# Sliding-window attention with sinks and a two-layer MLP on one core: the transpose of one pair moved from TensorE to the DMA, the second chunk's work in a new order, and attention slots placed one by one

## The chip, the cores and the metric

The kernel runs on one core of one Trainium2 chip. The metric is the device time in microseconds of one execution, as the median of several. The execution that the profile records has a *span* (first to last recorded instruction) that is about 2 us shorter than its device time; all times of a trace are counted from the span's start. Some executions run at a lowered TensorE clock; they are marked slow and no difference is read from them.

## The reference, cut to what matters

```python
scores = q @ k.T / sqrt(64)               # 4 batches, 8 heads, 768 tokens, 64 wide
keep = (key < 4) | (0 <= query - key < 128)      # 4 sinks, a window of 128
a = softmax(where(keep, scores, -1e9)) @ v
x = a.transpose(0, 2, 1, 3).reshape(3072, 512)
out = gelu(x @ w_in) @ w_out              # w_in 512 x 2048, w_out 2048 x 512
```

## The kernel before: the parts that matter

Tokens go in *pairs* of two blocks of 128 (pair 0 to 11); two pairs make a *chunk* of 512 tokens (0 to 5). For a chunk, gemm 1 multiplies x by W_in (gelu follows), and gemm 2 multiplies by W_out. While gemm 2 of one chunk runs, the attention of the next is put between its matmuls. For chunks 1 to 4 a loop does this. For chunk 0, with all the loads of the start, a list OPS written by hand says in which order all engines get their work; its last part is gemm 2 of chunk 0 with the attention of chunk 1 (pairs 2 and 3), called *the second chunk's attention* below.

```python
STREAM = [("k", 0), ("q", 0), ("v", 0), ("k", 1), ...]    # order of the loads; q, k, v of pairs 4 to 11 follow
OPS = [ ...
    ("T", [3,0], "V"), ("s", [2,2], ""), ("m", [2,2], ""), ("s", [2,3], ""),
    ("g2", [[0,6],[1,6],[0,7],[1,7]], ""), ("T", [3,1,1], "VA"), ("av", [2,0,2], ""),
    ("g2", [[0,8],[1,8],[0,9],[1,9]], ""), ("xT", [2,0], "V"), ("s", [3,0], ""),
    ... ]
```

"take" casts a loaded tile to bf16 (V = VectorE, A = ScalarE, G = GpSimd), "T" transposes q or k, "s" is one score with its exponential, "m" its mask on VectorE, "av" attention times v, "xT" the transpose of the attention output into x, "h" a quarter of gemm 1, "g2" four matmuls of gemm 2, "tab" a table load of ScalarE. A *filler* is a matmul whose result nobody uses; the *eviction* is the copy of finished output rows ("osb") out of the tile that the matmuls write.

A pair named in an "xT" gets its x by TensorE and a copy; any other by one crossbar transpose (a DMA transfer that transposes on its way) on the DMA queue of SyncE:

```python
    X_PE = {op[1][0] for op in OPS if op[0] == "xT"}
    ...
            if g in X_PE:                       # at the end of av
                PO[g, p] = po
            elif DONE[g] == NPAIR:
                o = 2 * (g % 2)
                nc.sync.dma_start(out=xt_tile(g // 2)[:, o : o + 2]..., in_=XG[g]..., transpose=True)
    ...
            elif name == "take":                # in run(OPS)
                take(tuple(args), *engs)
                pump(where["q", 6])             # issue loads up to pair 5's, as far as buffers are free
    ...
        n = 0                                   # chunks 1 to 4: where attention goes in
        LEAD = [6] + [8] * (len(att) - 2) + [10]
        for s in range(len(mms)):
            gemm2_mm(c, *mms[s])
            if n < len(att) and 2 * s >= 7 * n + LEAD[n]:
                for w in att[n]:
                    w()
                n += 1
```

Loads and crossbar transposes share one queue, so a transpose stands behind the loads issued before it.

The softmax here doesn't subtract the row's maximum and nothing guards it: scores larger than these inputs give would overflow.

## Time and profile before

225.46 us (median of 3, 225.24 to 225.54); with one more run at the time of the comparison, 225.35.

| Start of (us from the span's start) | before |
|---|---|
| first W_in matmul of chunk 0 | 21.43 |
| last W_in matmul of chunk 0 | 37.59 |
| first W_out matmul of chunk 0 | 38.92 |
| gemm 1 of chunks 1 to 5 | 59.99, 93.71, 126.47, 159.29, 192.78 |
| last copy of an output | 220.69 |
| end of the span | 223.60 |

The starts come from the single matmuls of the trace; the chain of waits starts a piece where the one before it ends, some 0.17 us later. TensorE is busy 96% of the span, so the table is a list of stages of one engine, and a gain is a stage that got shorter. The lines behind it stand in the prediction below.

### The profile page before, as it was taken

Reading aid. Unit: us, or ns where it says so; the run is one execution under the profiler, and the core shown is the slowest. Engines: PE = TensorE matmul, PEld = TensorE weight load, DVE = VectorE, ACT = ScalarE, POOL = GpSimd, SP = SyncE. Lnnn points to the kernel's source line nnn. Section 1 sums busy time; section 2 is a strip of 40 time slices with the busy share of each in tenths; the row PEclk is TensorE's granted clock in tenths of the full one; section 3 lists DMA queues with packets and bytes.
Section 4 is the critical chain, followed back from the end, with each engine's and each line's share of the span. In section 5 each row is a group of like instructions: output and inputs, shape, how many; then the busy total and the mean of one; then the engine's idle time right before and its main releaser. Section 6 shows DMA issues by size and latency. Waiting matters only on the chain.

```text
span 223.6 us, 4228 instructions
## 1 busy us (share of the span) xinstructions
PE 215.2 (96%) x1705; PEld 114.7 (51%) x1705; DVE 112.8 (50%) x267; ACT 120.8 (54%) x148; POOL 52.3 (23%) x97
## 2 busy tenths in 40 slices
PE   7798999999999999999999999999999999999994
PEld 2355887554544465444455444455444465444454
DVE  4438825887591188391188480288560297100121
ACT  2367675856255976055974065964156973177100
POOL 8475413546030011220011310011400011300100
PEclk9999999999999999999999999999999999999999
DMA  6999999999487995567995477996493026510022
GB/s 171 290 348 388 355 352 288 343 291 308 163 170 128 256 295 124 115 140 114 297 295 100 94 153 152 299 243 98 99 176 54 3 47 97 117 23 3 5 89 94
DMA packets 70066, 40.11 MB, mean 179 GB/s; under 512 B 27168, under 2 KB 64416, under 8 KB 70048
## 3 DMA queue, kind: packets, MB, share of 16 engines
q1 hardware_dynamic: 67824, 34.02, 61.4%
q0 software_dynamic: 2080, 5.77, 10.2%
q8 instruction: 13, 0.21, 0.4%
q10 hardware_dynamic: 144, 0.07, 0.1%
q14 instruction: 5, 0.04, 0.1%
HBM read 27.26 MB, written 6.29 MB: 150 GB/s over the span
## 4 chain that ended last, share of the span: by engine, by line
PE 85%; ACT 5%; DVE 4%; DMA 2%; issue 1%; SPq 0%; DVEq 0%
PE po L682 34%; PE big L613 29%; PE bank L546 4%; PE big L473 4%; PE big L646 4%; ACT et L482 3%; DMA st<-in_q_dram 2%; PE po L646 2%; PE bank L613 2%; PE bank L526 1%; ACT L715 1%; DVE et L490 1%; DVE xg L568 1%; PE qkps L363 1%; PE big L462 1%
## 5 line engine op out<-in xcount | busy, mean ns | idle before, releaser
L682 PE MATMUL po<-WOUT,gt 128*128 128x512 bf16 (+2 forms) x416 | 89.8, 364 | 0.1
L613 PE MATMUL big<-xt,WIN 128*128 128x512 bf16 x300 | 66.1, 379 | 0.0
L682 PEld LDWEIGHTS <-gt 128*128 128x128 bf16 x416 | 36.9, 98 | 38.9 <-issue 3.0
L632 ACT ACTIVATE gt<-big 128x1024 bf16<-128x1024 f32 (+1 forms) x32 | 30.6, 969 | 44.1 <-PE big L613 44.1
L613 PEld LDWEIGHTS <-WIN 128*128 128x128 bf16 x320 | 31.3, 98 | 37.8
L482 ACT ACTIVATE et<-big 128x1024 bf16<-128x1024 f32 (+1 forms) x48 | 43.4, 952 | 11.8 <-PE big L473 11.6
L697 POOL DMA_DIRECT2D out_dram<-osb x40 | 22.9, 578 | 107.8 <-DVE rz L564 79.9
L490 DVE TENSOR_TENSOR et<-et,mask 128x1024 bf16<-128x1024 bf16 x31 | 22.6, 739 | 33.6 <-ACT et L482 33.2
L272 DVE COPY osb<-po 128x512 f32<-128x512 f32 (+2 forms) x25 | 16.1, 645 | 39.2 <-PE po L682 39.2
L568 DVE TENSOR_TENSOR xg<-bank,rz 128x256 bf16<-128x256 f32 x44 | 18.7, 424 | 1.5
L546 PEld LDWEIGHTS <-et 128*128 128x128 bf16 x352 | 15.2, 97 | 4.9 <-DVE et L490 0.7
L272 DVE CAST vo<-st 64x512 bf16<-64x512 f32 x36 | 16.4, 457 | 0.4
L473 PE MATMUL big<-qt,kt 64*128 64x128 bf16 (+1 forms) x256 | 15.6, 238 | 0.8 <-ACT et L482 0.2
L546 PE MATMUL bank<-vo,et 128*128 128x65 bf16 x324 | 15.1, 193 | 0.6 <-DVE et L490 0.6
L626 ACT ACTIVATE gt<-big 128x1024 bf16<-128x1024 f32 (+1 forms) x8 | 9.8, 1243 | 10.7 <-PE big L613 10.7
L646 PEld LDWEIGHTS <-WIN 128*128 128x128 bf16 x128 | 12.3, 98 | 1.5
L473 PEld LDWEIGHTS <-kt 64*128 64x128 bf16 x256 | 8.6, 94 | 7.6 <-issue 6.0
L497 DVE TENSOR_TENSOR et<-et,mask 128x768 bf16<-128x768 bf16 x12 | 6.9, 579 | 10.0 <-ACT et L482 9.6
L715 ACT ACT_TABLE_LOAD x9 | 11.5, 1283 | 0.2
L646 PE MATMUL big<-xt,WIN 128*128 128x256 bf16 x80 | 10.3, 273 | 0.0
L564 DVE RECIPROCAL rz<-bank 128x4 f32<-128x4 f32 x44 | 7.7, 175 | 4.6 <-PE bank L546 3.8
L272 DVE CAST k<-st 128x1024 bf16<-128x1024 f32 (+1 forms) x12 | 8.0, 669 | 3.3 <-DMA st<-in_k_dram 3.2
(87 smaller groups left out, 142.8 us busy)
## 6 DMA issues: line engine op xcount, KB each, us to landing
st<-in_k_dram SPq DMA_DIRECT2D x12, 512.0 KB, 7.3
st<-in_q_dram SPq DMA_DIRECT2D x12, 512.0 KB, 7.2
st<-in_v_dram SPq DMA_DIRECT2D x12, 512.0 KB, 7.2
out_dram<-osb POOLq DMA_DIRECT2D x40, 128.0 KB, 2.7
st<-in_moe_w_in_dram SPq DMA_DIRECT2D x8, 512.0 KB, 9.4
st<-in_moe_w_out_dram SPq DMA_DIRECT2D x8, 512.0 KB, 8.8
out_dram<-osb POOLq DMA_DIRECT2D x2, 256.0 KB, 2.3
kt<-k SPq DMA_TRANSPOSE x16, 3.0
```

The lines of the kernel that those rows point to most:

```text
L272: eng.tensor_copy(out=out, in_=in_)
L473: nc.tensor.matmul(ps[:, hl, c : c + n * P], lhsT=kt(gk, p, ek, rows), rhs=qt(g, p, e, n, rows), start=not add, stop=True, skip_group_chec ...
L482: nc.scalar.activation(out=et[:, :, c0:], in_=ps[:, :, c0:], func=AF.Exp, scale=att_scale)
L490: nc.vector.tensor_tensor(out=et.rearrange("p h (e n) -> p (h e) n", e=2), in0=et.rearrange("p h (e n) -> p (h e) n", e=2), in1=mask.unsqu ...
L546: nc.tensor.matmul(pos[n][:, e * PV + hl * DV : e * PV + (hl + 1) * DV], lhsT=ets[n][:, hl, c : c + P], rhs=vo[:, h, :], start=e == 0 and ...
L568: nc.vector.tensor_tensor(out=XG[g][:, :, 2 * p : 2 * p + 2, :], in0=po[:, 0 : 2 * PV].rearrange("p (e h c) -> p e h c", e=2, h=2)[:, :, : ...
L613: nc.tensor.matmul(outs[a], lhsT=WIN[:, t, ts(f, P)], rhs=XT[c][:, :, t, :], start=(t == 0), stop=(t == NKT - 1),)
L632: nc.scalar.activation(out=gt.rearrange("k a n -> k (a n)"), in_=src, func=AF.Gelu)
L646: nc.tensor.matmul(out4[a], lhsT=WIN[:, t, ts(f, P)], rhs=XT[c][:, 2 * half : 2 * half + 2, t, :], start=(t == 0), stop=(t == NKT - 1), sk ...
L682: nc.tensor.matmul(po, lhsT=GT[c, f // 4][:, f % 4, ts(m, P)], rhs=WOUT[:, f, cols], start=(f == 0), stop=(f == NFT - 1),)
L697: nc.gpsimd.dma_start(out=out[r0 : r0 + P, :].rearrange("(s r) c -> r s c", r=2)[r], in_=osb[HP * r : HP * (r + 1), :],)
L715: nc.scalar.activation(out=warm[:, 1:2], in_=warm[:, 0:1], func=func)
```

## The change

Its intent: eight transposes less for TensorE, and fewer moments in which it waits in the second chunk's attention and at the later chunks' scores. The diff without most of the reordered list:

```diff
 STREAM = [
-    ("k", 0), ("q", 0), ("v", 0), ("k", 1), ("q", 1), ("v", 1), ("wi", 0), ("wi", 1), ("wi", 3),
+    ("k", 0), ("q", 0), ("v", 0), ("k", 1), ("q", 1), ("wi", 0), ("v", 1), ("wi", 1), ("wi", 2),
...
-    ("wo", 1), ("wo", 0), ("k", 2), ("v", 2), ("q", 3), ("k", 3), ("wo", 4), ("wo", 5),
+    ("wo", 2), ("k", 2), ("wo", 0), ("q", 3), ("v", 2), ("k", 3), ("wo", 4), ("wo", 5),
 OPS = [
... (the head: other engines for casts and copies, two products later)
-    ("T", [3,0], "V"), ("s", [2,2], ""), ("m", [2,2], ""), ("s", [2,3], ""),
-    ("g2", [[0,6],[1,6],[0,7],[1,7]], ""), ("T", [3,1,1], "VA"), ("av", [2,0,2], ""),
-    ("g2", [[0,8],[1,8],[0,9],[1,9]], ""), ("xT", [2,0], "V"), ("s", [3,0], ""),
+    ("T", [3,0], "V"), ("s", [2,2], ""), ("g2", [[0,4],[1,4],[0,5],[1,5]], ""),
+    ("s", [2,3], ""), ("m", [2,2], ""), ("g2", [[0,6],[1,6],[0,7],[1,7]], ""),
+    ("T", [3,1,1], "V"), ("g2", [[0,8],[1,8],[0,9],[1,9]], ""), ("av", [2,0,2], ""),
... (("xT", [2,0..3]) are gone)
+    SLOT = [3, 12, 19, 26, 33, 41]
+    def ahead():
+        return where["q", 6 if 2 in X_PE or DONE.get(2) == NPAIR else 5]
...
-                pump(where["q", 6])
+                pump(ahead())
...                                            (after av)
+                pump(ahead())
...
-        n = 0
-        LEAD = [6] + [8] * (len(att) - 2) + [10]
-        for s in range(len(mms)):
-            gemm2_mm(c, *mms[s])
-            if n < len(att) and 2 * s >= 7 * n + LEAD[n]:
-                for w in att[n]:
+        for n, mm in enumerate(mms):
+            gemm2_mm(c, *mm)
+            if att and n in SLOT:
+                for w in att[2 * SLOT.index(n)]:
                     w()
-                n += 1
```

`ahead()` holds the loads of pair 5 until the transpose of pair 2 has been issued. The old loop's filled slots lay after matmuls 3, 11, 18, 25, 32 and 40.

## The prediction

> **What bounds the kernel now.** I read the page first, then the table of stretches, the chain of waits in order of time, what the matmuls waited for, and last the timelines of single engines around the waits found.
>
> ```profile
> PE 215.2 (96%) x1705; PEld 114.7 (51%) x1705; DVE 112.8 (50%) x267; ACT 120.8 (54%) x148; POOL 52.3 (23%) x97
> L613 PE MATMUL big<-xt,WIN 128*128 128x512 bf16 x300 | 66.1, 379 | 0.0
> ```
>
> Only TensorE is full. But 379 ns for a 128x512 matmul is not its cost: matmuls overlap. The chain gives the true price, 32 of them in 6.91 us, so 216 ns each. With that price I went through the starts of all matmuls of the trace and counted as lost only what exceeds columns/2.4 GHz + 2.5 ns.
>
> ```profile
> 7.00:15.00 8.00, 7.23 (x83) 4.20 (x83) 4.20 (x10) 4.36 (x7) 4.99 (x9) 1.00 1.17 309
> 15.00:24.00 9.00, 8.01 (x99) 5.29 (x94) 6.39 (x15) 6.91 (x10) 5.54 (x7) 1.00 1.05 387
> 24.00:37.50 13.50, 13.50 (x150) 12.16 (x149) 6.18 (x14) 8.16 (x13) 4.42 (x5) 1.00 1.10 327
> 37.50:60.16 22.66, 21.82 (x209) 11.55 (x207) 16.40 (x38) 14.57 (x23) 9.78 (x14) 1.00 0.99 296
> 60.16:74.20 14.04, 14.04 (x66) 6.34 (x65) 7.68 (x15) 7.65 (x8) 2.63 (x4) 1.00 0.74 137
> ```
>
> Columns: length, then busy time of TensorE, its weight loads, VectorE, ScalarE, GpSimd, then clock, DMA share (over 1 where packets overlap), GB/s. From 24 us on TensorE has hardly a hole; gaps are at the start (7 to 24 us), in the second chunk's attention (37.5 to 60) and, small, at the head of later attention stages:
>
> ```profile
> 37.46 0.70 DVE kt L272
> 38.21 0.56 PE big L473 x10
> ...
> 43.62 1.41 DVE et L490
> 45.07 0.41 PE bank L546 x8
> ...
> 51.10 0.61 DVE osb L272
> 51.75 0.81 PE po L682 x3
> ...
> 76.34 1.83 ACT et L482 x2
> 78.22 0.40 PE big L473 x6
> ...
> 142.73 1.93 ACT et L482 x2
> 144.69 0.40 PE big L473 x6
> ```
>
> Each non-PE piece here is the work whose end releases the matmul below it. Between starts the losses are: 0.36 us at 38.21 (the copy of k), 0.15 at 43.64 (a transpose beginning), 0.75 at 45.07 (the mask of the last score), 0.23 at 51.75 (eviction of the first two output rows, "osb"). In the later chunks the second score of the second slot waits for the exponentials of the first slot: 0.28, 0.13, 0.39 and 0.28 us at 78.22, 111.50, 144.69, 177.29. The last 30.7 us (from 192.94) have no hole and the change does not touch them.
>
> **What the Trainium skill says.** "Perfetto Trace Analysis", introduction: matmul busy time is a poor measure because matmuls are pipelined. Agreed: 379 ns reported, 216 ns paid. "TensorE: Matmul & The Clock Gate", section "Wait — 56ns, not 53.3ns?": warm matmuls start every N / 2.4 GHz + about 2.5 ns, 215.7 ns at N=512; the chain's 216 ns agrees and its 128-column price of 56 ns prices the transposes below. "TensorEngine Tiling (Array Packing)", "Key Properties": a change of tiling mode drains the array. The trace shows about 0.09 to 0.10 us at nearly each step between the 64-row score matmuls and 128-row ones. "DMA: Bandwidth & Descriptors", "Anatomy of one DMA": a semaphore wait is served by the issuing sequencer, so a transfer that must wait blocks those behind it. That is why the loads of q, k, v for pair index 5 are now held until the transpose of x for pair index 2 is issued.
>
> **The change part by part.**
>
> (1) Pair 2's x no longer passes TensorE: four "xT" go, which are 8 transposes of 128 columns (rows of line L588), 8 x 56 ns = 0.45 us of TensorE, and four copies (0.28 us on VectorE, 0.37 on ScalarE), which are off the path. One crossbar transpose takes their place on the DMA. Its cost is latency:
>
> ```profile
> 89.80 1.24 SPq L579 DMA_TRANSPOSE xt<-xg  x1
> ...
> DMA to landing us min/median/max: 3.0/3.1/4.5
> ```
>
> In the changed order the second half of pair 2's attention output follows the matmuls of output rows 0 and 1, by my count near 50.2 us; with 0.9 us of VectorE and up to 4.5 us of DMA, x lands at about 55.7, and gemm 1 of chunk 1 wants it near 58.8. Hidden. The held loads then issue near 53; before, three took from 48.42 to a last landing near 60.6, so they end near 61 to 62, while their casts start after those of pair 4, at about 63. Hidden too.
>
> (2) New order of the second chunk's attention. k of pair 2 is streamed two places earlier (about 1.8 us sooner), so the 0.36 us at 38.21 goes. Masks move ahead: the first attention product now has four W_out matmuls more before it (0.86 us), so the 0.75 and 0.15 us should go. Fewer separate score clusters save perhaps one switch, 0.1. The eviction wait of 0.23 stays: ScalarE still reaches that copy late. With the 0.45 of (1) this removes 0.36 + 0.75 + 0.15 + 0.10 + 0.45 = 1.8 us. It adds a wait: only 8 W_out matmuls (1.73 us) and a 0.45 us transpose now stand between the first two scores and the third, while ScalarE has its second gelu (end 38.6), the table load 1.28, the sink weights 0.39 and one exponential 0.97, up to about 41.2; TensorE arrives at 41.0: 0.25 us lost. Net 1.55. But a DMA floor comes next: the last W_out load.
>
> ```profile
> 35.14 3.20 SPq L259 DMA_DIRECT2D st<-in_moe_w_out_dram  x4
> ...
> 48.56 1.05 ACT L270 CAST WOUT<-st 128x1024 bf16<-128x1024 f32 x1
> ```
>
> It is issued at 37.9 and lands 8.9 us later, at 46.8, and the stream is bandwidth-bound up to there, so no reordering brings it sooner. ScalarE can cast it from about 47.3 to 48.4. Its matmuls started at 49.80 before; they cannot start before 48.4. I therefore count 1.2 us for this stage and the start together.
>
> (3) The start. The casts and copies are dealt out anew and v1 is loaded after the first W_in. By walking the new order with the old durations, the first score still starts at 9.57 (the filler matmuls set it), the score of pair 1 some 0.35 us later (its q copy starts on the slower ScalarE, and two more fillers of 512 columns stand before it), and the sink weights about 1 us later, because ScalarE now casts a W_in tile (1.04 us) between exponentials. Against that, v of pair 0 is used later and two attention products move behind other work. First W_in matmul: between 20.9 and 21.9 us, 21.43 before. I take zero, with 0.5 us either way.
>
> (4) Slots. Before, the filled slots fell after matmuls 3, 11, 18, 25, 32, 40 of each chunk's 64; now 3, 12, 19, 26, 33, 41. One 216 ns matmul moves ahead of the waiting score, so of each wait up to 0.216 is filled: 0.216 + 0.134 + 0.216 + 0.216 = 0.78 us over four chunks. Nothing else changes its spacing. The price is that the last transpose of x is issued 0.216 us later: it landed near 92.8 (89.80 + 3.0) where gemm 1 began at 93.87, the smallest such margin being about 0.8 us. Still hidden. I count 0.75.
>
> Sum: 1.2 + 0 + 0.75 = 1.95 us. 225.46 - 1.95 = 223.5.
>
> **Rivals.**
> - *A pure TensorE count.* If only removed work counts, the gain is 0.45 us: 225.0. Against it: the holes listed are real, and the change puts work into each.
> - *The start gets worse.* Should the later sink weights delay the first W_in matmul by 0.5 to 1 us and ScalarE, with two more casts of 1.04 us in the gelu stage, hold buffers that TensorE wants, (2) and (3) come to 0.3 and the time to 224.4. For it: ScalarE would be busy for some 13.5 of 16 us there (gelu 4 x 1.02 and 8 x 0.54, a table load 1.28, three casts 3.1, copies 0.75). Against: gelu of each tile still has a tile of slack.
> - *The crossbar is late, or the held loads are.* Then gemm 1 of chunk 1 starts on a wait and 1 to 3 us are lost: 225 to 227. The margin of about 3 us speaks against it.
> - *All holes close and the start gains too*, because the W_out floor is softer than I think: 1.55 + 0.5 + 0.78, so 222.6.
>
> **Range and chances.** The certain part is small, the spread comes from the start and the W_out floor: 222.6 to 224.5. Two per cent is 4.5 us; the holes that exist between 7 and 192 us outside the fillers are hardly more than that, so faster by over 2% has 0.01. Slower by over 2% needs a new stall of 4.5 us: 0.01.
>
> **What would show it.** (1) right: eight TensorE instructions of line L588 less, a transpose of x issued near 51 and landed before 57, no wait of gemm 1 for a DMA near 59. (2): no wait of the attention product on a mask; a wait of about 0.25 us for the exponential near 41; gemm 1 of chunk 1 starting at 58.7 to 59.0 instead of 60.0. (3): first W_in matmul at 21.4. (4): chunks 1 to 4 each about 0.2 us shorter from start to start (33.7, 32.8, 32.8, 33.5 before). It is wrong if a DMA or ScalarE shows up as what TensorE waits for anywhere after 55 us, or if the start moves by over 0.6 us.

## The result, and the profile after

222.90 us (median of 4 runs, 222.76 to 222.91) against 225.35: the ratio is 0.9897 with a 95% interval of 0.9872 to 0.9922, a real gain of about 1%. A ratio here is the mean time of one kernel's fast runs over that of the other's of the same rounds, so not quite the ratio of the medians quoted. The range of 222.6 to 224.5 held it; the point, 223.5, was 0.6 us too high.

| Start of (us) | before | after | difference |
|---|---|---|---|
| first W_in matmul | 21.43 | 20.32 | -1.11 |
| last W_in matmul | 37.59 | 37.07 | -0.52 |
| first W_out matmul | 38.92 | 38.04 | -0.88 |
| gemm 1 of chunk 1 | 59.99 | 57.70 | -2.29 |
| gemm 1 of chunk 5 | 192.78 | 189.71 | -3.07 |
| last copy of an output | 220.69 | 217.62 | -3.07 |
| end of the span | 223.60 | 220.85 | -2.75 |
| time of that execution | 225.31 | 222.91 | -2.40 |

The last two rows already say something not foreseen: of 3.07 us gained on the engines, 0.67 is given back after the last copy.

The page of the changed kernel, its first part:

```profile
PE 214.6 (97%) x1699; PEld 114.5 (52%) x1699; DVE 108.5 (49%) x264; ACT 123.7 (56%) x149; POOL 51.9 (24%) x97
```

TensorE has six matmuls fewer (eight transposes gone, two filler matmuls more) and only 0.6 us less busy time. The rest of the gain is idle time that went. Its table of stretches, cut at the corresponding places (columns as in the prediction):

```profile
7.00:15.00 8.00, 7.45 (x79) 4.20 (x79) 3.45 (x8) 5.17 (x8) 4.17 (x7) 1.00 1.17 310
15.00:24.00 9.00, 8.40 (x117) 5.80 (x117) 8.03 (x20) 8.02 (x10) 4.82 (x6) 1.00 1.05 386
...
37.10:57.87 20.77, 20.44 (x200) 10.98 (x198) 14.12 (x37) 13.20 (x19) 10.09 (x14) 1.00 1.09 290
```

The last of these was 22.66 us with 21.82 busy; it is 20.77 with 20.44 busy: TensorE idles 0.33 us instead of 0.84. The chain of waits over it, in order of time:

```profile
39.37 0.39 ACT ets L440
39.76 0.92 ACT et L482
40.72 0.40 PE big L473 x6
...
44.70 0.48 PE bank L546 x16
...
49.67 1.83 PE po L682 x8
...
57.00 0.86 PE po L682 x4
57.87 6.91 PE big L613 x32
...
75.69 0.64 PE big L473 x12
```

The mask (DVE et) before the attention product at 44.70 and the eviction (DVE osb) before the W_out matmuls at 49.67 are gone, as is the copy of k before the first score. This is the line of that mask before, and below it that of the same mask in e1_slots, an experiment whose kernel is the same up to there:

```profile
43.62 1.40 DVE L490 TENSOR_TENSOR et<-et,mask 128x1024 bf16<-128x1024 bf16 x1 [0.43 <-ACT et L482]
```

```profile
43.28 0.97 DVE L490 TENSOR_TENSOR et<-et,mask 128x1024 bf16<-128x1024 bf16 x1 [0.43 <-ACT et L482]
```

In both, GpSimd casts a W_out tile when the mask begins (until 44.48 and 43.71 us), and the mask ends 0.54 us after that cast. In the changed kernel the mask before the attention product takes 0.70 us, at 43.05.

What is left is the third score at 40.72, which waits for an exponential. The second slot's scores at 75.69 follow matmuls without a wait. The table of waits agrees (three of its lines):

```profile
PE big L473 <- ACT et L482: 0.3, 1, 0.3
PE big L646 <- DVE xt L272: 0.2, 1, 0.2
PE big L646 <- ACT xt L270: 0.2, 1, 0.2
```

It gives the wait at 40.72 as 0.3; from the starts of the matmuls I count 0.40 (0.50 less the 0.10 of the step from 128-row to 64-row matmuls). The two waits of L646 are the second and third groups of the first W_in matmuls, which wait for x of pair 0 (0.35 and 0.38 us by the starts).

The new transpose, from the timeline of SyncE's queue, and where its result is wanted, from TensorE's:

```profile
45.89 1.65 SPq L247 DMA_DIRECT2D st<-in_v_dram  x1
50.76 2.32 SPq L579 DMA_TRANSPOSE xt<-xg  x1
53.17 0.53 SPq L247 DMA_DIRECT2D st<-in_q_dram  x1
```

```profile
57.70 2.54 PE L613 MATMUL big<-xt,WIN 128*128 128x512 bf16 x11
```

```profile
DMA to landing us min/median/max: 3.0/3.1/6.5
```

The last line covers the nine crossbar transposes of x; its maximum is the new one. Issued at 50.76 it landed at 57.30, 0.40 us before gemm 1. The held loads of pair 5 follow it at once and land by 62.33, hidden. The transpose itself is hidden too, in this profile narrowly; in the profiles of e0_after, e3_newtail, e7_mask_later, e8_best and e9_v4held the margin was 0.7 to 1.9 us.

### The profile page after: what moved, and what is told of

Same layout as the page of the kernel before. It is cut to its first block, busy times and chain, and to the rows that moved or that the text cites.

```text
span 220.9 us, 4215 instructions
## 1 busy us (share of the span) xinstructions
PE 214.6 (97%) x1699; PEld 114.5 (52%) x1699; DVE 108.5 (49%) x264; ACT 123.7 (56%) x149; POOL 51.9 (24%) x97
## 4 chain that ended last, share of the span: by engine, by line
PE 90%; ACT 3%; DMA 2%; DVE 2%; issue 1%; SPq 0%
PE po L682 38%; PE big L613 29%; PE big L473 5%; PE bank L546 4%; PE big L646 4%; DMA st<-in_q_dram 2%; PE po L646 2%; PE bank L613 2%; PE bank L526 1%; ACT et L482 1%; PE big L408 1%; PE big L363 1%; DVE et L490 1%; PE qkps L363 1%; ACT L440 1%
## 5 line engine op out<-in xcount | busy, mean ns | idle before, releaser
L490 DVE TENSOR_TENSOR et<-et,mask 128x1024 bf16<-128x1024 bf16 x31 | 22.0, 717 | 33.8 <-ACT et L482 33.2
L272 DVE CAST vo<-st 64x512 bf16<-64x512 f32 x36 | 15.7, 437 | 2.0 <-DMA st<-in_v_dram 1.6
L473 PE MATMUL big<-qt,kt 64*128 64x128 bf16 (+1 forms) x256 | 15.0, 238 | 0.4 <-ACT et L482 0.3
L646 PEld LDWEIGHTS <-WIN 128*128 128x128 bf16 x128 | 12.2, 98 | 2.0 <-issue 0.4
L646 PE MATMUL big<-xt,WIN 128*128 128x256 bf16 x80 | 10.5, 272 | 0.4 <-DVE xt L272 0.2
L272 POOL CAST vo<-st 64x512 bf16<-64x512 f32 x12 | 8.4, 697 | 7.5 <-DMA st<-in_v_dram 7.0
L272 DVE CAST k<-st 128x1024 bf16<-128x1024 f32 (+1 forms) x11 | 7.2, 656 | 4.1 <-DMA st<-in_k_dram 4.0
```

Source lines behind the costliest of these rows:

```text
L272: eng.tensor_copy(out=out, in_=in_)
L473: nc.tensor.matmul(ps[:, hl, c : c + n * P], lhsT=kt(gk, p, ek, rows), rhs=qt(g, p, e, n, rows), start=not add, stop=True, skip_group_chec ...
L490: nc.vector.tensor_tensor(out=et.rearrange("p h (e n) -> p (h e) n", e=2), in0=et.rearrange("p h (e n) -> p (h e) n", e=2), in1=mask.unsqu ...
L646: nc.tensor.matmul(out4[a], lhsT=WIN[:, t, ts(f, P)], rhs=XT[c][:, 2 * half : 2 * half + 2, t, :], start=(t == 0), stop=(t == NKT - 1), sk ...
```

## The experiments

All kernels were correct. Each was timed with 5 rounds (e9_v4held 3) against the kernel before. Kernels are compared only within the same rounds. That kernel's medians in the three calls were 224.57, 225.04 and 225.17 us, its runs between 224.01 and 225.39.

### The slots alone

The kernel before with SLOT = [3, 12, 19, 26, 33, 41]:

```diff
-    SLOT = [3, 11, 18, 25, 32, 40]     (the old loop, written out)
+    SLOT = [3, 12, 19, 26, 33, 41]
```

> The kernel before with the new slots alone (3, 12, 19, 26, 33, 41 in place of 3, 11, 18, 25, 32, 40). If the slots are worth what the filled waits are (theory: one 216 ns matmul in front of each of four waiting scores), chunks 1 to 4 shrink by 0.21, 0.13 to 0.15, 0.21, 0.21 us and the kernel by about 0.78 us, ratio 0.9965. If the wait only moves to another score or to the transpose of x at the chunk's end (rival), the chunks keep their lengths and the ratio is 1.000.

Measured: 223.79 us (223.64 to 224.54), ratio 0.9962 (0.9942 to 0.9983). From one gemm 1 start to the next the chunks take 33.50, 32.62, 32.60 and 33.28 us, where they took 33.71, 32.77, 32.81 and 33.49: 0.78 us together, and the same four numbers stand, within 0.01 us, in the changed kernel. The theory holds.

### The new head alone

The kernel before with the new STREAM and the new OPS up to the last gelu of chunk 0; the rest old, pair 2 by TensorE:

```diff
 STREAM, OPS up to ("gelu", [3,1])      as in the changed kernel
 OPS behind it, SLOT                    as in the kernel before
```

> The new load order and the new order of operations up to the end of chunk 0's gemm 1, then the old order of the second attention, old slots, x of pair 2 by TensorE. Theory that the start has a gain of its own which I had taken for zero: the last W_in matmul comes 0.5 us earlier (37.1 in place of 37.6), W_out starts near 38.0 in place of 38.9, and most of that 0.5 to 0.9 us reaches the end, ratio about 0.997. Rival: the second stage is tied to the landing of W_out and to ScalarE, so that an earlier start is eaten there and the ratio is within 0.001 of 1.

Measured: 224.51 us (224.04 to 225.08), ratio 0.9993 (0.9968 to 1.0018). The first W_in matmul starts at 20.37, the last at 37.08, the first W_out matmul at 38.05. That is the head of the changed kernel. The wait for the copy of k is gone, and of the 0.75 us for the mask 0.15 is left. Yet the time shows almost nothing. One reason is that the executions of the kernel before are themselves of two kinds. In the profile of e1_slots, whose instructions up to gemm 1 of chunk 1 are the same as before, the first W_in matmul started at 20.54 and the last at 37.24: the new head is then ahead by 0.16 at the last W_in matmul, not 0.52. There the mask costs 0.32 us, not 0.75, and gemm 1 of chunk 1 starts at 59.23, so e2_newhead (58.46) is ahead by 0.77 and not by 1.53. Its own runs lie at two levels too (224.04 to 224.13 and 224.89 to 225.08). The other reason is that this kernel's time exceeds its span by 2.03 to 2.09 us, that of e1_slots by only 1.68 to 1.74; I found no cause for this.

### The new second chunk's attention alone

```diff
 STREAM, OPS up to ("gelu", [3,1]), SLOT     as in the kernel before
 OPS behind it, crossbar, held loads         as in the changed kernel
```

> The old start, then the new order of the second attention with the transpose of pair 2's x on the crossbar and the loads held, old slots. Theory: the stage from the first W_out matmul to gemm 1 of chunk 1 takes 19.7 us in place of 21.1, so 1.4 us less, ratio 0.9938, whatever the start did. Rival: part of the stage's gain was lent by the earlier start (more time for k and for the masks); then it is under 1 us here.

Measured: 223.99 us (223.50 to 224.10), ratio 0.9963 (0.9944 to 0.9983). From the first W_out matmul to gemm 1 of chunk 1 it takes 19.55 us, where the kernel before took 21.07: 1.52 less, from this part. Of this, 0.43 is the mask's longer wait (0.75, not 0.32); against the 20.65 us of e1_slots it is 1.10. The theory's stage came (19.55 for 19.7), its ratio did not (0.9963, not 0.9938): a part of the gain is lost again behind the last copy, of which below. The three parts alone give 0.38%, 0.07% and 0.37%, together 0.82%, near the 0.93 to 1.03% of the whole.

### The crossbar in the old order

```diff
-("xT", [2,0], "V") ... ("xT", [2,2], "V") ... ("xT", [2,1], "A"), ("xT", [2,3], "A")
+pump(ahead()) in place of pump(where["q", 6]), and after av
```

> The kernel before with the crossbar for pair 2's x and the hold alone, old order, old slots. Theory: 0.45 us less, ratio 0.998, gemm 1 of chunk 1 0.45 us earlier than in the same state of the kernel before (59.2 or 60.0), the transpose landing by 57 or 58 and hidden. Rival: the transpose lands behind the start of gemm 1, and the ratio is 1.00 or above.

Measured: 225.66 us (224.95 to 225.83), ratio 1.0022 (1.0005 to 1.0039): slower. The same stage takes 20.84 us instead of 21.07, 0.23 less and not 0.45. The chain shows why:

```profile
50.86 0.61 DVE osb L272
...
51.51 0.81 PE po L682 x3
```

The four transposes of TensorE that stood there had covered part of the time in which the first output rows are evicted; without them the wait for the eviction is longer (two waits of 0.35, with the step between matmul forms in it, and 0.23 us there, one of 0.23 before). And everything after the last copy takes longer, of which below.

### The new order with pair 2 on TensorE

```diff
     ("g2", [[0,10],[1,10],[0,11],[1,11]], ""),
+    ("xT", [2,0], "V"), ("xT", [2,2], "A"),
     ("m", [2,1], ""), ...
     ("g2", [[2,0],[3,0],[2,1],[3,1]], ""),
+    ("xT", [2,1], "V"), ("xT", [2,3], "A"),
     ("tab", ["Gelu"], ""),
```

> The changed kernel with the x of pair 2 transposed by TensorE again (eight more transposes in the new order, two behind each of the attention products, their copies on VectorE and ScalarE), no hold of loads. If TensorE's own time is all that the crossbar saves: 8 x 56 ns = 0.45 us more, gemm 1 of chunk 1 at 58.1 to 58.2 in place of 57.7. If the copies and the longer holding of the PSUM banks count too (rival): 0.8 us or more, with a wait for a bank or a copy in the stage.

Measured: 223.84 us (223.26 to 224.31), ratio 0.9950 (0.9931 to 0.9969), about 0.96 us slower than the changed kernel. Gemm 1 of chunk 1 starts at 58.70, 1.00 us later than with the crossbar. The chain has a wait that the changed kernel lacks:

```profile
49.80 0.48 ACT osb L270
...
50.33 1.02 PE po L682 x4
```

ScalarE, which has the eviction of the first rows and now a copy of x, comes to it late (0.25 us lost), a transpose waits at 46.66 (0.20 us), and at 48.35 the W_out matmuls of the last tile wait 0.16 us: ScalarE's cast of that tile, which stands behind the copy of x, ends at 48.30. The rival's account holds. The loads of pair 5 are not held here either, so two things differ; no wait of TensorE in this stage names a load. So eight transposes of 0.45 us cost 1.00 in the new order, and saved 0.23 when taken out of the old one (there with the hold). Their worth is the holes around them, not their own length. (The 1.00 is between two profiles; from that of e0_after below, which has another wait, it would be 0.34. But the medians of six runs differ by 0.96, and from the last copy to the end of the reported time it takes 5.2 and 5.3 us in the two, so about 1.0 stands. In this profile the last output also took 2.27 us to land instead of 1.56, so its end is not compared.)

### The loads of pair 5 not held

```diff
-        return where["q", 6 if 2 in X_PE or DONE.get(2) == NPAIR else 5]
+        return where["q", 6]
```

> The changed kernel without the hold: the loads of pair 5 may be issued before the transpose of pair 2's x. Theory that the hold is what makes the crossbar affordable: the transpose is issued behind three loads, lands near 60 us or later in place of 57.3, gemm 1 of chunk 1 waits for it and the kernel takes 2 to 4 us more than the changed one, ratio to the kernel before about 1.00 to 1.007. Rival: the transpose is issued at the same time anyway because the three loads are issued by 54, and it only lands a little later; then gemm 1 starts within 0.5 us of 57.7.

Measured: 226.86 us median of all (225.80 to 229.84, one slow), ratio 1.0090 (1.0053 to 1.0127): worse than the kernel before. The chain:

```profile
53.26 8.23 DMA xt<-xg
...
61.53 8.75 PE big L613 x32
```

and the table of stretches from the start of gemm 1 of chunk 1:

```profile
61.50:65.10 3.60, 3.57 (x9) 1.28 (x9) 3.27 (x7) 0.15 (x1) 0.00 (x0) 0.53 1.07 220
65.10:70.00 4.90, 4.90 (x24) 2.28 (x23) 0.00 (x0) 2.92 (x3) 0.00 (x0) 0.99 0.69 122
```

Behind three loads more, whose issues follow one another from 47.95 to 53.16 us though x is ready at 50.41, the transpose is issued 2.5 us later and takes 8.2 us; TensorE waits 3.8 us for it. Then its clock is 0.53 for 3.6 us: the same 32 matmuls take 8.75 us in place of 6.91. "TensorE: Matmul & The Clock Gate", section "HAM oscillation — how this bites in real kernels", warns of idle gaps over about 3.4 us, and the trace agrees: a wait of 3.8 us cost 1.7 us more in chunk 1 (35.18 us long, not 33.50). Not every execution loses the clock: two of the six took 225.80 and 225.91 us at mean clocks of 0.998 and 1.0, where the profiled one (228.44 us) had 0.991. The hold is what makes the crossbar usable here.

### One load more held

```diff
-        return where["q", 6 if 2 in X_PE or DONE.get(2) == NPAIR else 5]
+        return where["q", 6] if 2 in X_PE or DONE.get(2) == NPAIR else where["v", 4]
```

> The changed kernel with one load more held, that of v of pair 4, so that the crossbar transpose of pair 2's x has no load in front of it. If its 6.5 us to landing are the queue in front of it (the v load landed at 52.8, two us after the transpose was issued), it lands near 54 to 55 in place of 57.3; the time stays at the changed kernel's 222.9, for it was hidden by 0.4 us. If the slowness is of the stage's other traffic (rival), it still lands after 56.5.

Measured: 222.80 us (222.40 to 223.15, 4 runs), ratio 0.9897 (0.9877 to 0.9917), the same as the changed kernel. The transpose was issued at 50.82 and landed at 56.37, after 5.6 us. That is 1.0 us less than in the first profile of the changed kernel, and still far from the 3.1 us of the quiet chunks. But in e0_after, the same changed kernel with the load in front, it took 5.70 us too (51.42 to 57.12), and 5.1 to 6.2 in other kernels with that load (e3_newtail, e6_oldorder_xbar, e7_mask_later). So no effect of the load directly in front is shown. That the excess comes from other traffic of the DMA engines is my reading; no run isolates it.

### The changed kernel again

> The changed kernel once more, beside the variants of this batch, since the kernel before has shown two levels near 224.3 and 225.2 us. Theory that the two levels come from one mask multiplication on VectorE in the start that either goes ahead of a GpSimd cast or waits it out: here the mask at 19.4 us takes 1.5 us in some executions and 0.7 in others, and the time is 222.9 where it waits, 222.5 where not. Rival (the levels are the chip's): a mask of 0.7 us comes with the same 222.9.

Measured: 222.88 us (222.47 to 223.54), ratio 0.9907 (0.9890 to 0.9924). Its profile, of the slowest of the six runs, shows a wait that the first profile did not have:

```profile
42.84 1.45 POOL WOUT L272
...
44.33 1.02 PE po L682 x4
```

A W_out tile (the fifth, "wo4") landed at 42.79, where it landed at 41.89 in the first profile, and GpSimd's cast of it took until 44.28. TensorE lost 1.02 us. Gemm 1 of chunk 1 started at 58.36. So the loads of W_out do limit this stage, in some executions. The theory is not confirmed: the mask, at 19.51, took 0.68 us, its fast case, and the last W_in matmul came 0.36 us earlier than in the first profile, but this execution was the slowest of the six.

### The mask behind the copies of x

The two waits at the first W_in matmuls are for copies of x that stand behind a mask on VectorE:

```diff
     ("s", [1,2], ""), ("xT", [0,3], "V"),
-    ("m", [1,1], ""), ("xT", [0,2], "V"), ("xT", [0,1], "A"), ("m", [1,2], ""),
+    ("xT", [0,2], "V"), ("xT", [0,1], "V"), ("m", [1,1], ""), ("m", [1,2], ""),
```

> The changed kernel with one mask multiplication of the start moved behind two copies of x on VectorE, and one of those copies moved from ScalarE to VectorE. If the first W_in matmuls wait (0.35 and 0.38 us) for copies that stand behind the mask and behind an exponential, both waits go, the last W_in matmul is at 36.4 to 36.7 in place of 37.1, and 0.4 to 0.7 us less arrive at the end: near 222.3. Rival: the crossbar transpose of pair 2, which lands at 57.3 whatever the start does, then becomes what gemm 1 of chunk 1 waits for, and under 0.3 us is gained.

Measured: 222.70 us (222.38 to 223.62), ratio 0.9904 (0.9886 to 0.9922). Both waits are gone, the last W_in matmul starts at 36.70 and gemm 1 of chunk 1 at 57.34, 0.36 us earlier than in the first profile. But the second profile of the changed kernel had its last W_in matmul at 36.71 as well. In the time the two can't be told apart. The rival's wait did not come (the transpose landed at 56.62, 0.72 us before gemm 1), though the median gained only 0.18 us.

### The same mask in the kernel before

```diff
     ("sv", [0], "C"),
-    ("m", [1,0], ""), ("av", [0,2], ""), ... ("av", [0,1], "CW8"), ("xT", [0,3], "A"),
+    ("av", [0,2], ""), ... ("av", [0,1], "CW8"), ("m", [1,0], ""), ("xT", [0,3], "A"),
```

> The kernel before with one VectorE mask multiplication of the start moved behind two pairs of reciprocal and multiplication, so that it no longer starts in the same 30 ns as a GpSimd cast. Theory that the two levels of the kernel before come from that race: only the lower level is left, all runs near 224.3 to 224.6, first W_in matmul at 20.5, ratio about 0.997. Rival (levels of the chip or of the DMA): both levels stay, first W_in matmul at 20.5 or 21.4.

Measured: five fast runs, 223.97 to 224.78 us, ratio 0.9976 (0.9958 to 0.9994); the sixth, 368.67 us at a clock of 0.563, is slow, and the profile fell into it. Two levels remain (223.97 and 224.15; 224.64 to 224.78). The race told at the end of this document can be a part of the two kinds, but not the only cause. A candidate for the rest, untested, is the same race at the mask of the second chunk's attention (waits of 0.75 and 0.32 us), which this edit does not move. This is left open.

### Towards a better version

e7_mask_later with the fourth pair's v held as well, and the second slot of chunk 3 one place later (0.17 us of its wait was left):

```diff
-            if att and n in SLOT:
+            at = SLOT if c != 3 else [3, 13, 19, 26, 33, 41]
+            if att and n in at:
```

> The mask moved behind the copies of x, the v load held, and in chunk 3 the second slot after matmul 13 in place of 12. Each part removes a wait that a trace showed: 0.36 us in the executions in which the mask waits for GpSimd, 0.17 us of chunk 3 (32.60 to 32.43), and the risk of a late transpose. Expected 222.4 to 222.6, ratio about 0.989; if the landing of the W_out tiles is the floor (rival), the start's part is lost in a wait for a W_out cast near 43 us and it is 222.7 to 222.9.

Measured: four fast runs, 222.30 to 223.20 us, ratio 0.9903 (0.9883 to 0.9923); the profile fell into a slow run. Nothing gained that can be seen; the mean of 222.8 is in the rival's range, but without a fast profile its reason can't be checked.

The same, with four W_out matmuls ahead of the wait left at 40.72:

```diff
+    ("g2", [[0,4],[1,4],[0,5],[1,5]], ""),
     ("T", [3,0], "V"), ("s", [2,2], ""),
-    ("g2", [[0,4],[1,4],[0,5],[1,5]], ""), ("s", [2,3], ""), ("m", [2,2], ""),
-    ("g2", [[0,6],[1,6],[0,7],[1,7]], ""),
+    ("g2", [[0,6],[1,6],[0,7],[1,7]], ""), ("s", [2,3], ""), ("m", [2,2], ""),
```

> The same, and in the second attention four W_out matmuls moved in front of the score that waits 0.4 us for ScalarE's exponential. If that wait is lost time, another 0.4 us goes, 222.1. If the landing of the fifth and later W_out tiles is the floor (my reading), TensorE waits about as long for their casts between 42.5 and 44 us, and the time is that of the run before within 0.1 us.

Measured: 222.18 us (222.08 to 222.33, 4 runs), ratio 0.9876 (0.9859 to 0.9892): the fastest kernel, and the only one that stays below all runs of e9_v4held. Its gemm 1 of chunk 1 starts at 57.17. The number of the theory came, its mechanism only in part: the wait did not vanish; it moved from the third score to the transposes of k behind it, where 0.35 us is left:

```profile
41.68 0.94 ACT et L482
...
42.66 0.61 PE big L363 x8
```

I had expected the W_out loads to eat this gain; in its profile TensorE waited for none. Chunk 3 took 32.53 us instead of 32.60.

## Why the prediction was right or wrong, point by point

**(4), slots: right.** 0.75 to 0.78 us predicted, 0.78 measured alone and within the whole.

**(3), the start: the first matmul missed, the end of the start about right.** The first W_in matmul came at 20.32, outside the 20.9 to 21.9 foretold, and moved by 1.11 us, more than the 0.6 that the prediction itself named as a sign of being wrong. Two new waits behind it (0.35 and 0.38) took most of that back: at the last W_in matmul the profiles differ by 0.52 us. The kernel before has a faster kind of start, caught in e1_slots, and against that one the changed kernel gains 0.22 at the first (20.54 to 20.32) and 0.17 at the last (37.24 to 37.07). The single profile of before that I worked from showed the slower kind; its times (225.24 to 225.54) were all of the upper level too, while later runs went down to 224.01.

**(2), the second chunk's attention: the waits went as said, but terms were mis-sized and the cap was wrong.** The wait for k (0.36) went; k was streamed one place earlier, not two, and landed 1.5 us sooner. The stage behind it became 1.41 us shorter; the prediction's own terms without k (0.75, 0.15, 0.10 and 0.45, less 0.25) give 1.20. But the 0.75 for the mask was that of an execution in which the mask waited for a cast of GpSimd; in e1_slots it was 0.32, and against that profile the stage became 0.99 us shorter. The added wait was 0.40 rather than 0.25. The eviction wait of 0.23, which I said would stay because of ScalarE, went. In the kernel before ScalarE was idle when its copy became due (50.66); it was VectorE's copy that came late (51.02). In the new order an attention product and a score stand between those output rows and the next, and VectorE's copy starts at 48.84. In e5_xpe, with copies of x on ScalarE too, a wait for ScalarE's copy appears. The failing step was the cap: "I therefore count 1.2 us for this stage and the start together". I took the landing of the last W_out tile at 46.8 as fixed. It landed at 45.99, its cast ended at 47.41, its matmuls began at 47.78 where I had put 48.4 as the earliest, and nothing waited for it. (In e0_after these were 47.09, 48.16 and 48.43, so the cap was near there, but cost nothing.) The tile that can limit is an earlier one, wo4, and only in some executions (1.02 us in e0_after). Without the cap the prediction's net for this stage was 1.55. The gain up to gemm 1 of chunk 1 was 2.29 us against the one profile of before and 1.53 against e1_slots (59.23), 0.17 of it from the start; that 1.53 is so near to 1.55 is in part luck, for terms were wrong both ways.

**(1), the crossbar: hidden, as said, but both numbers were off.** It was issued at 50.76 as predicted ("near 51") and landed at 57.30, 6.5 us later, not 4.5 at most; gemm 1 also came earlier than I thought. The margin was 0.40 us (0.7 to 1.9 in the five other profiles named above), not 3. The latencies that I used came from chunks in which few loads run; this one runs among them. And 0.45 us was not its worth: 0.23 in the old order, 1.00 in the new. The parts are not additive, because in the old order the transposes filled holes that exist anyway.

**Not foreseen: a cost at the end.** In every kernel with pair 2 on the crossbar, from the landing of the last output to the end of the span it takes 1.33 to 1.35 us, in the others 0.92 to 1.03. At the end SyncE goes through the same nine semaphore waits before and after, in a fixed order, about 0.06 us apart. Its transfers take eight semaphores in turn, and with one transfer more (88, not 87) the last output has the one that is waited for early in that order: seven more waits come behind it. Before, its was the last of the nine. So the first drain comes 0.08 us after the last output landed before, 0.52 after. From the last copy to the end this is 3.23 us in place of 2.91. In addition the time exceeds the span by 2.01 to 2.12 us in the changed kernel (1.75 to 2.14 in its variants with the crossbar), where the kernel before, e1_slots, e5_xpe and e11_before_mask have 1.66 to 1.78. e2_newhead has the larger difference without the crossbar (2.03 to 2.09), so the crossbar is not its only source; its cause stays open. Together that is 0.67 us of 3.07. Without it the time would have been near 222.2, below the range: that the range held is in part luck, a gain larger than foretold and a cost not foretold.

**The rivals.** The pure count of TensorE work (225.0) fell, as did the bad start. The late crossbar fell for the changed kernel and came true as soon as the loads were not held (e4_nohold). "All holes close and the W_out floor is softer", 222.6, was nearest to what happened: 3.07 us gained in the profiles, of which 0.76 is the kind of the one profile of before (59.99 against 59.23: 0.34 up to the first W_out matmul, 0.42 behind it, the longer wait for the mask), and 0.67 given back at the end.

## What to carry to other kernels

Price work that is moved off a full engine by what stands around it in the order, not by its own length: the same eight transposes were worth 0.23 us in one order and 1.00 in another. A transfer put into a stage full of loads should be given the latency of that stage, and the loads that would stand in front of it should be held back; here the wait otherwise was 3.8 us and cost the clock as well. Before a gain of one per cent is split into parts, look at more than one execution of both kernels, since one profile can show waits (0.76 us here) that other executions do not have.

## What the Trainium skill lacked or had wrong

- *"GPSIMD Engine Reference", section "1. Specifications"*: it says that GpSimd shares its SBUF interfaces with VectorE, with contention where a VectorE instruction has two SBUF inputs. The traces agree. The page has no size, but this is no gap of the whole skill, whose page on the SBUF goes further on which of the two waits; what the runs add is the price in this kernel. The mask multiplication (two SBUF inputs, 128x1024 bf16) takes 0.68 us alone. In the profile of before it began at 17.81 while GpSimd cast two W_in tiles:

```profile
17.81 1.54 DVE L490 TENSOR_TENSOR et<-et,mask 128x1024 bf16<-128x1024 bf16 x1
```

```profile
16.79 2.02 POOL L272 CAST WIN<-st 128x1024 bf16<-128x1024 f32 x2
```

  In e1_slots, with the same instructions up to there:

```profile
17.79 0.68 DVE L490 TENSOR_TENSOR et<-et,mask 128x1024 bf16<-128x1024 bf16 x1
```

```profile
16.80 2.57 POOL L272 CAST WIN<-st 128x1024 bf16<-128x1024 f32 x2
```

  One of the two waits for the other (VectorE 0.86 us longer, or GpSimd 0.55), and the starts of the two lay within 0.03 us of each other in both profiles, so small shifts decide which. The mask of the second chunk's attention did the same in these two profiles (1.40 and 0.97 us) and held up TensorE by 0.75 and 0.32. In the changed kernel the mask at 19.47 took 1.54 us in one profile, 0.68 in the next, and GpSimd's cast then 1.43 instead of 1.04.
- *"VectorE: DVE Perf Modes", section "The three transpose paths"*: it gives 1309 ns for a 128x128 transpose by the DMA crossbar, and nothing on what other transfers do to it. No page has this. Here a 128x1024 bf16 one took from issue to landing 3.0 to 3.1 us in most cases of the later chunks and up to 4.7 in the others, 5.1 to 6.5 beside the loads of the second chunk's attention, and 8.2 with three loads more in front.
- *"Runtime: NRT & Kernel Launch", section "The ~15µs preamble/postamble breakdown"*: it calls the gap between the profile's total and the reported time the same for all kernels, with a range of 6.02 to 6.67 us over 14 of them. The runs do not show this to be wrong: the span used here is another measure (shorter than the time), and its distance from the time varied less than that range, 1.68 to 1.76 us in e1_slots and e5_xpe, 2.01 to 2.12 in the changed kernel. But at a gain of 1% a difference of 0.35 us counts.
- No page has the cost at the end of a program of semaphores that a queue must still wait for: about 0.06 us for each one here, and 0.3 us in all where the last output's semaphore is waited for early in the order and not last. That one more transfer on the queue moved it there is read from the semaphores in the traces (all kernels with 88 transfers of SyncE have it, none with 87); no run changed the count alone.
